# Five conv taps as four sums, some of them on GpSimd, with two heads in adjacent banks and an issue order written out

## The chip, the core and the metric

The kernel runs on one core of a Trainium2 chip. A core has TensorE (PE, with its weight loads shown apart as PEld), VectorE (DVE), ScalarE (ACT), GpSimd (POOL), and SyncE (SP), whose queue issues the DMAs. Each engine runs its own instructions in order; semaphores make one wait for another. The metric is device time in microseconds (us), the median of several runs. Next to it stands one profiled execution, from which all durations come.

## The reference

Batch 8, 8 heads, sequence 576, head width 64, all float32. Attention with a decay, then a gated linear unit whose gate is a causal convolution of five taps per channel:

```python
cum = np.cumsum(np.maximum(s, 0.0), axis=-1)
bias = -(cum[:, :, :, None] - cum[:, :, None, :])
scores = np.where(causal, -1000000000.0, scale * q @ k.T + np.minimum(bias, 0.0))
attn = softmax(scores)
x = (attn @ v)                       # heads side by side: (8, 576, 512)
for kk in range(5):
    gate_pre += conv_w[kk] * xp[:, kk:kk + S, :]      # xp: x with 4 zero rows in front
gate = 1.0 / (1.0 + np.exp(-gate_pre))
out = (gate * (x @ w_val)) @ w_out
```

## The kernel before

The work is cut into 32 steps n = 4b + p: batch b, and p, a pair of heads, which is also one chunk of 128 of the 512 channels. The decay factors into a weight on each row of v: `w = exp(cum - half)` multiplies v and a column of ones (`Vp`), so the scores need only exp and the causal mask, and the ones column gives the softmax denominator.

For one pair: `qk_T` transposes the bf16 q and k on TensorE and `qk_evac` (L516) copies them to `QKT`. `scores` (L521) computes the lower triangle in three steps of 512 columns (`STEPS`), each head in a bank of its own. In step 0, the diagonal blocks, four more matmuls with `sel` and `futA`/`futB` add -30000 above the diagonal (L563). `exps` (L566) runs one exp per head and step, from PSUM to `P` in bf16. `av` (L576) multiplies by `Vp`; `norm` takes two reciprocals (L583) and two products (L585), one of each per head. `x_T` transposes the result to channels by tokens in a PSUM bank, `x_evac` (L598) copies it to `xT` (four zero columns in front).

Then the convolution, `tap` (L600 to L612): tap 0 writes `gp = x * cwT[4]` over 576 columns, on DVE (L609) or, for odd n, on ACT (L607); taps 1 to 4 add `x` shifted by 1 to 4 columns times the other weights, all on DVE (L611), reading x from its PSUM bank. `tanh` (L616) gives the gate, `val` (L636) multiplies `xT` by `w_val`, `glu` (L642) forms `(tanh + 1) * val`, `outp` (L648) multiplies by half of `w_out`, `out_evac` (L653) copies to SBUF on ACT, and `store` writes out.

POOL builds constants at the start; later it casts q and k of batches 1 to 7 (L473) and their last 64 rows (L688), and multiplies Vp of these batches (L483). For batch 0 DVE and ACT do these steps. `w_val` and `w_out` are cast on DVE (L438).

The order comes from a planner, `Plan.run`: every task is added with an engine, an estimated duration, a due time (`DUE`), what it depends on and which buffers it takes (8 PSUM banks, 3 `P`, 2 `gp`, 6 `th`, 3 `ot`, 3 `qkf`). The planner simulates the five engines, picks for each the ready task that is due first, and the instructions are issued in the order that it finds. All DMAs go through SP's queue. At the end a small check counts rows whose softmax denominators are in range; unless all 128 are good, a second, general path runs as well.

Of the kernel before, what the change touches and what calls it, by code (L numbers as in the profile page):

```python
# [17 lines left out]
DM = 512  # L18
# [185 lines left out]
def pcol(kb, qb):  # L204
    if kb == qb:
        return kb * 128
    if qb == 4:
# [13 lines left out]

DUE = dict(av=1.08, norm=-15.2, xt=1.96, xe=-1.95, tap=2.26, dtap=0.21, tanh=3.88, cpe=-1.58, val=4.62,
           dval=0.97, out=12.49, dout=0.2, oute=12.42, qt=-3.05, qe=4.97, tt=-2, te=-24.47, s4=0.17,
           vp=-16.42, cast=4.1, lqk=-10.33, lv=-7.3)

STAY = (0.28, 13.36)

ON_PE = ()  # L230
PE_CHUNK = 2

ON_ACT = tuple(range(1, 32, 2))


class Plan:

    LAG = 0.2  # L240
    SWITCH = 0.18

    def __init__(self, bufs):
        self.bufs = bufs
        self.tasks = []
        self.slot = {}

    def add(self, eng, us, key, emit, deps=(), take=(), give=(), mode="N"):
        t = dict(eng=eng, us=us, key=key, emit=emit, deps=[d for d in deps if d is not None], take=take,
                 give=give, mode=mode, n=len(self.tasks), done=None)  # L250
        self.tasks.append(t)
        return t

    def run(self):
        engs = ["SP", "POOL", "PE", "ACT", "DVE"]
        free = {k: [(0.0, i) for i in range(n)] for k, n in self.bufs.items()}
        idle_at = dict.fromkeys(engs, 0.0)
        ready = {e: [] for e in engs}
        after = [[] for _ in self.tasks]
        for t in self.tasks:  # L260
            t["at"] = 0.0
            names = {d["n"] for d in t["deps"]}
            t["left"] = len(names)
            for i in names:
                after[i].append(t)
            if not names:
                ready[t["eng"]].append(t)
        mode, dma_free, now = "N", 0.0, 0.0
        self.order = []

        def can(t):

            at = t["at"]
            for kind in {kind for kind, _ in t["take"]}:
                c = sum(other == kind for other, _ in t["take"])
                if len(free[kind]) < c:
                    return None
                at = max(at, sorted(free[kind])[c - 1][0])
            return at

        while len(self.order) < len(self.tasks):
            started, later = False, []
            for e in engs:
                if idle_at[e] > now + 1e-9:
                    later.append(idle_at[e])
                    continue
                pick = None
                for t in ready[e]:
                    at = can(t)
                    if at is None:  # L290
                        continue
                    if at > now + 1e-9:
                        later.append(at)
                        continue
                    key = t["key"] + (STAY[t["mode"] == "N"] if e == "PE" and t["mode"] != mode else 0)
                    if pick is None or (key, t["n"]) < pick[:2]:
                        pick = (key, t["n"], t)
                if pick is None:
                    continue
                t = pick[2]  # L300
                us = t["us"]
                if e == "PE" and t["mode"] != mode:
                    us += self.SWITCH
                    mode = t["mode"]
                for kind, tok in t["take"]:
                    got = min(free[kind])
                    free[kind].remove(got)
                    self.slot[kind, tok] = got[1]
                t["start"] = now
                if e == "SP":  # L310
                    idle_at[e] = now + 0.06
                    dma_free = max(dma_free, now + 1.2) + us
                    t["done"] = dma_free + 0.8
                else:
                    idle_at[e] = t["done"] = now + us
                for kind, tok in t["give"]:
                    free[kind].append((t["done"] + self.LAG, self.slot[kind, tok]))
                ready[e].remove(t)
                self.order.append(t)
                later.append(idle_at[e])  # L320
                started = True
                for o in after[t["n"]]:
                    o["at"] = max(o["at"], t["done"] + (self.LAG if o["eng"] != e else 0.0))
                    o["left"] -= 1
                    if o["left"] == 0:
                        ready[o["eng"]].append(o)
            if not started:
                assert later
                now = min(later)
        return max(t["done"] for t in self.order)  # L330


def main_path(ctx, tc, q, k, v, s, moe_w_val, moe_conv_w, moe_w_out, out, okcnt):

# [5 lines left out]
    plan = Plan(dict(m=8, P=3, gp=2, th=6, ot=3, qkf=3))  # L343
    add, slot = plan.add, plan.slot

    def work(kind, tok, shape, dt):
        return one.tile(shape, dt, name=f"{kind}{slot[kind, tok]}")

    def bank(tok, shape, dt=FP32):
        return psum.tile(shape, dt, name=f"m{slot['m', tok]}")  # L350

    PE_CONV = lambda b, c: b in ON_PE and c == PE_CHUNK
    NS = B * 4

# [5 lines left out]
    vst = one.tile([128, NKB, 8, 65], FP32, name="vst")  # L360
    nc.gpsimd.memset(vst[:, :, :, 64:65], 1.0)
    nc.gpsimd.memset(vst[0:64, 4, :, :], 0.0)


    sel = one.tile([128, 2, 128], BF16, name="sel")
    nc.gpsimd.memset(sel, 0.0)
    futA = one.tile([128, 4, 64], BF16, name="futA")
    futB = one.tile([128, 4, 128], BF16, name="futB")
    nc.gpsimd.memset(futA, 0.0)
    nc.gpsimd.memset(futB, 0.0)  # L370
    for r0 in (0, 64):
        r = slice(r0, r0 + 64)
        for j in range(2):
            nc.gpsimd.tensor_copy(sel[r, j, 64 * j:64 * j + 64], ident[r, r])
        nc.gpsimd.affine_select(out=futA[r], in_=futA[r], pattern=[[0, 4], [1, 64]], compare_op=ALU.is_ge,
                                fill=NEG, base=0, channel_multiplier=-1)
        nc.gpsimd.affine_select(out=futB[r], in_=futB[r], pattern=[[0, 4], [1, 128]], compare_op=ALU.is_ge,
                                fill=NEG, base=-64, channel_multiplier=-1)
    P4s = [one.tile([128, 2, 4, 128], BF16, name=f"P4{j}") for j in range(2)]
    for P4 in P4s:  # L380
        nc.gpsimd.memset(P4[:, :, :, 0:64], 0.0)


    two = lambda name, shape, dt: [one.tile(shape, dt, name=f"{name}{j}") for j in range(2)]
    qkbs = [two("qb", [128, 4, 512], BF16), two("kb", [128, 4, 512], BF16)]
    tails, tailbs = two("tail", [128, 512], FP32), two("tailb", [128, 512], BF16)
    QKTs = two("QKT", [128, 2, 4, S], BF16)
    Vps = two("Vp", [128, NKB, 8, 65], BF16)
    xns = two("xn", [128, NKB, 512], BF16)
    xTs = two("xT", [128, 4, 4 + S], BF16)  # L390
    glus = two("glu", [128, 4, S], BF16)
# [9 lines left out]
    dg = one.tile([128, 15, 128], BF16, name="dg") if ON_PE else None  # L401
    for xT in xTs:
        nc.vector.memset(xT[:, :, 0:4], 0.0)


    t_s = add("SP", 0.8, -9, lambda: nc.sync.dma_start(out=sp, in_=s.rearrange("b h s -> (b h) s")))

    def relu():
        nc.vector.tensor_scalar(sp, sp, 0.0, None, ALU.max)

    def total():
        nc.vector.tensor_tensor_scan(cum, sp, sp, 0.0, ALU.add, ALU.max)

    def centre():
        nc.vector.tensor_scalar(chalf, cum[:, S - 1:S], 0.5, None, ALU.mult)  # L415
        nc.vector.tensor_scalar(cum, cum, chalf, None, ALU.subtract)

    def decay_T():
        pt = bank("w", [128, NKB, 64])
        slot["w"] = pt  # L420
        for i in range(NKB):
            nc.tensor.transpose(pt[:, i, :], cum[:, WIN[i]:WIN[i] + 128], identf)

    t = add("DVE", 0.65, -8, relu, [t_s])
    t = add("DVE", 1.3, -8, total, [t])
    t = add("DVE", 0.75, -8, centre, [t])
    t = add("PE", 1.2, -8, decay_T, [t], take=[("m", "w")])
    t_w = add("ACT", 0.5, -8, lambda: nc.scalar.activation(out=w, in_=slot["w"], func=AF.Exp), [t],
              give=[("m", "w")])


    t_wvo = []
    for nm, src, dst, sc, key in (("wv", moe_w_val, wv, 1.0, -5), ("wo", moe_w_out, wo, 0.5, -2.4)):
        def load(nm=nm, src=src):
            wt = slot[nm] = work("qkf", nm, [128, 4, DM], FP32)
            nc.sync.dma_start(out=wt, in_=src.rearrange("(c p) d -> p c d", c=4))
# [5 lines left out]
    def conv_T():  # L442
        pt = slot["cw"] = bank("cw", [128, 4, 5])
        for c in range(4):
            nc.tensor.transpose(pt[:, c, :], cw[:, c * 128:(c + 1) * 128], identf[0:5, 0:5])
# [416 lines left out]
```

## Time and profile before

| what | us |
|---|---|
| median of 3 runs (lowest to highest) | 227.53 (227.32 to 229.33) |
| span of the profiled execution | 228.0 |
| TensorE's mean granted clock there | 0.927 of full speed |

The profiled execution lies half a microsecond above the median. A profile page gives, for each engine, its busy time and share of the span, and the span in 40 slices, a digit being the busy tenths of a slice. Groups of instructions are given by line, engine and operation, with output and inputs by the program's names, shapes, count, busy time, the mean length of one, and the idle time of the engine just before them with what ended it. The chain of waits starts at the last instruction and goes back, at each step, to whatever released it. Instructions of an engine overlap at their ends, so a group's busy time is less than count times mean.

### The profile page before, as it was taken

The numbers are of one execution on the slowest core, as the hardware profiler recorded it, in microseconds if no ns is written. First come the engines' busy times: TensorE is split into PE (matmuls) and PEld (weight loads), VectorE is DVE, ScalarE is ACT, GpSimd is POOL, SyncE is SP. The second block draws the span as 40 slices with busy tenths as digits, with TensorE's granted clock in tenths as the row PEclk, the third lists the DMA queues.
The fourth block names the chain that finished last, engine by engine and source line by source line (L and its number), as shares of the span: only waits on it lengthen the run. The fifth ranks groups of instructions, "written<-read, shape, count | busy, mean of one in ns | idle before, by whom it ended". The sixth has DMA issues, their size and how long they took to land.

```text
span 228.0 us, 6320 instructions
## 1 busy us (share of the span) xinstructions
PE 194.5 (85%) x2561; PEld 129.0 (57%) x2561; DVE 190.3 (83%) x390; ACT 189.0 (83%) x348; POOL 73.4 (32%) x73
## 2 busy tenths in 40 slices
PE   0859876986999999998999699999999999899580
PEld 0547563573846756575657356765666566656220
DVE  3444459999899999999989979899899999999800
ACT  3698899925899999989999889899999989965340
POOL 8500622553873004959121770005305200000000
PEclk9965997697699999999999889999999999999887
DMA  5999999999994999599459121194291041044242
GB/s 152 240 274 329 270 170 299 298 176 195 358 249 141 207 325 297 155 253 377 175 131 267 45 69 49 35 203 135 115 230 29 3 184 26 3 159 162 96 149 74
DMA packets 69231, 40.50 MB, mean 178 GB/s; under 512 B 47109, under 2 KB 63493, under 8 KB 69194
## 3 DMA queue, kind: packets, MB, share of 16 engines
q1 hardware_dynamic: 69194, 40.01, 66.2%
q8 instruction: 22, 0.36, 0.6%
q14 instruction: 15, 0.12, 0.2%
HBM read 30.57 MB, written 9.44 MB: 175 GB/s over the span
## 4 chain that ended last, share of the span: by engine, by line
DVE 69%; PE 12%; SPq 8%; DMA 6%; issue 2%; ACT 1%; ACTq 0%
DVE gp L611 38%; DVE xn L585 10%; DVE glu L642 8%; DVE gp L609 5%; DMA qkf<-in_moe_w_val_dram 4%; DVE xT L598 4%; PE m L636 3%; PE m L648 3%; SPq L470 3%; SPq L478 2%; DVE recs L583 2%; SPq L489 2%; PE m L512 2%; PE m L576 1%; DMA out_dram<-ot 1%
## 5 line engine op out<-in xcount | busy, mean ns | idle before, releaser
L566 ACT ACTIVATE P<-m 128x512 bf16<-128x512 f32 x192 | 104.4, 672 | 11.0 <-PE m L563 9.1
L611 DVE SCALAR_TENSOR_TENSOR gp<-m,cwT,gp 128x572 f32<-128x572 bf16 (+3 forms) x128 | 102.9, 810 | 2.0
L521 PE MATMUL m<-QKT 64*128 64x128 bf16 (+4 forms) x576 | 45.8, 253 | 9.5 <-DVE xn L585 2.9
L483 POOL TENSOR_TENSOR Vp<-vst,w 128x650 bf16<-128x650 f32 x28 | 35.0, 1281 | 45.9 <-DMA vst<-in_v_dram 40.6
L636 PE MATMUL m<-xT,wv 128*128 128x288 bf16 x256 | 41.3, 293 | 2.8 <-DVE xn L585 0.8
L648 PE MATMUL m<-wo,glu 128*128 128x512 bf16 x160 | 41.9, 397 | 1.0 <-DVE gp L611 0.3
L521 PEld LDWEIGHTS <-QKT 64*128 64x128 bf16 x576 | 21.7, 98 | 31.4 <-issue 18.8
L576 PE MATMUL m<-Vp,P 128*128 128x65 bf16 x960 | 37.6, 197 | 1.8 <-ACT P L566 1.4
L576 PEld LDWEIGHTS <-P 128*128 128x128 bf16 x960 | 35.1, 100 | 5.6 <-ACT P L566 1.6
L516 ACT COPY QKT<-m 128x1024 bf16<-128x1024 bf16 x32 | 33.4, 1069 | 5.6 <-PE m L512 5.4
L653 ACT COPY ot<-m 128x512 f32<-128x512 f32 (+1 forms) x40 | 25.1, 651 | 9.4 <-PE m L648 6.7
L636 PEld LDWEIGHTS <-wv 128*128 128x128 bf16 x256 | 23.7, 99 | 13.8 <-issue 6.1
L642 DVE SCALAR_TENSOR_TENSOR glu<-th,m 128x288 bf16<-128x288 f32 x64 | 27.6, 445 | 1.4 <-PE m L636 1.4
L585 DVE TENSOR_TENSOR xn<-m,recs 128x320 bf16<-128x320 f32 x64 | 28.2, 482 | 0.0
L616 ACT ACTIVATE th<-gp 128x576 f32<-128x576 f32 x32 | 24.5, 767 | 1.6 <-DVE gp L611 1.6
L648 PEld LDWEIGHTS <-glu 128*128 128x128 bf16 x160 | 15.1, 101 | 18.1 <-issue 6.3
L473 POOL CAST qb<-qkf 128x2048 bf16<-128x2048 f32 x7 | 13.2, 1893 | 24.4 <-DMA qkf<-in_q_dram 16.2
L512 PE MATMUL m<-ident,qb 128*128 128x128 bf16 x128 | 13.9, 238 | 8.2 <-DVE chalf L415 6.1
L598 DVE COPY xT<-m 128x576 bf16<-128x576 bf16 x32 | 14.3, 449 | 5.1 <-PE m L594 5.1
L512 PEld LDWEIGHTS <-qb 128*128 128x128 bf16 x128 | 9.7, 107 | 11.7 <-DVE chalf L415 6.1
L594 PE MATMUL m<-ident,xn 128*128 128x128 bf16 x160 | 15.2, 230 | 1.1 <-ACT P L566 0.7
L473 POOL CAST kb<-qkf 128x2048 bf16<-128x2048 f32 x7 | 13.3, 1894 | 4.4 <-DMA qkf<-in_k_dram 4.4
(58 smaller groups left out, 154.1 us busy)
## 6 DMA issues: line engine op xcount, KB each, us to landing
out_dram<-ot SPq DMA_DIRECT2D x32, 256.0 KB, 2.2
qkf<-in_q_dram SPq DMA_DIRECT2D x7, 1024.0 KB, 9.8
qkf<-in_k_dram SPq DMA_DIRECT2D x7, 1024.0 KB, 9.0
vst<-in_v_dram SPq DMA_DIRECT2D x28, 256.0 KB, 5.0
vst<-in_v_dram SPq DMA_DIRECT2D x15, 128.0 KB, 4.6
first<-in_q_dram SPq DMA_DIRECT2D x4, 256.0 KB, 3.9
first<-in_k_dram SPq DMA_DIRECT2D x4, 256.0 KB, 4.0
tail<-in_q_dram SPq DMA_DIRECT2D x8, 128.0 KB, 9.3
```

The lines of the kernel that those rows point to most:

```text
L473: eng(qkbs[which][b % 2].rearrange("p j (h d) -> p h j d", h=8)[:, hs], f.rearrange("p h (j d) -> p h j d", j=4))
L483: eng.tensor_tensor(Vps[b % 2][:, :, h], vst[:, :, h], w[:, :, b * 8 + 2 * p:b * 8 + 2 * p + 2].unsqueeze(3).to_broadcast([128, NKB, 2, 65 ...
L512: nc.tensor.transpose(pt[:, which, j * 128:(j + 1) * 128], qkbs[which][b % 2][:, j, p * 128:(p + 1) * 128], ident)
L516: nc.scalar.copy(QKTs[b % 2][:, :, p, 0:512].rearrange("d w (x j) -> d w x j", j=4), slot["qt", b, p].rearrange("d w (j x) -> d w x j", j=4))
L521: nc.tensor.matmul(ps[hh][:, c0:c0 + nq], QKTs[b % 2][r, 1, p, k0:k0 + 128], QKTs[b % 2][r, 0, p, q0:q0 + nq], **kw)
L566: nc.scalar.activation(out=slot["Pt", n][:, hh, step * 512:(step + 1) * 512], in_=slot["s", n, step][hh], func=AF.Exp, scale=0.125)
L576: nc.tensor.matmul(ps[:, qb * 65:qb * 65 + 65], lhsT, Vps[b % 2][:, kb, 2 * p + hh, :], start=(kb == 0), stop=(kb == qb))
L585: nc.vector.tensor_tensor(xns[b % 2][:, :, p * 128 + hh * 64:p * 128 + hh * 64 + 64], pvs[hh][:, :, 0:64], recs[:, n, hh].unsqueeze(2).to_ ...
L611: nc.vector.scalar_tensor_tensor(gp[:, sh:S], x[:, 0:S - sh], cwT[:, c, 4 - sh:5 - sh], gp[:, sh:S], ALU.mult, ALU.add)
L636: nc.tensor.matmul(ps, wv[:, dc, c * 128:(c + 1) * 128], xTs[b % 2][:, dc, 4 + o:4 + o + 288], start=(dc == 0), stop=(dc == 3))
L642: nc.vector.scalar_tensor_tensor(glus[b % 2][:, c, o], slot["t", n][:, o], 1.0, slot["v", n, hf], ALU.add, ALU.mult)
L648: nc.tensor.matmul(ps, glus[b % 2][:, c, WIN[i]:WIN[i] + 128], wo[:, c, :], start=(c == 0), stop=(c == 3))
```

## The change

The planner, its due times and its buffers by name go. An `ORDER` text of tokens `step.indices:engine:slots` takes their place: the engine is S, G (GpSimd), T (TensorE), A or V, and the slots name PSUM banks and buffers. A loop issues the steps in this order. Loads, casts and evictions may name any engine.

```diff
-DUE = dict(av=1.08, norm=-15.2, xt=1.96, xe=-1.95, tap=2.26, dtap=0.21, tanh=3.88, cpe=-1.58, val=4.62,
...
-ON_ACT = tuple(range(1, 32, 2))
-class Plan:
...
+BUFS = {'vst': 1, 'P': 3, 'gp': 4, 'th': 5, 'ot': 4, 'qkf': 3, 'qkw': 2048}
+ORDER = """
...
+t3.7:G ld_v.3.3:S s1.10:T:6 rec.8:V nm.8:V val.6.1:T:1 e1.10:A ld_v.3.2:S s2.10:T:2 oe.0.2:V:0 xt.8:T:4 e2.10:A
+mk.10:G glu.6.1:V s0.11:T:6:2 ld_v.3.0:S val.7.0:T:5 xe.8:V e0.11:A t1.8:V:0 s1.11:T:0 st.0.2:S s2.11:T:2 ld_q.4:S:0
...
+t1.30:V:2 st.6.0:S t2.30:V out.6.3:T:2 oe.6.1:A:3 st.6.1:S xe.31:V out.6.4:T:1 th.29:A:0 t3.30:G t1.31:V:0
+oe.6.3:A:0 out.6.2:T:0 t2.31:V oe.6.4:A:1 st.6.3:S val.30.0:T:2 st.6.4:S t4.30:G oe.6.2:A:2 t3.31:V val.30.1:T:1
...
+"""
+    with tc.manual_schedule():
+        for name, e, *slots in steps:
+            f, *ix = name.split(".")
...
+            does[f](engines[e], *ix)
```

The weights of the convolution become ratios to the last one, whose half becomes the scale of tanh. A sum on GpSimd is two instructions, since GpSimd reads `xT` from SBUF and has a product and an addition apart:

```diff
+    def conv_ratio(e):
+        vec.tensor_copy(cwT, bank[:, at["cwT"][0], 0:20].rearrange("p (c k) -> p c k", c=4))
+        vec.reciprocal(cwi, cwT[:, :, 4:5])
+        vec.tensor_tensor(cwr[:, :, 0:4], cwT[:, :, 0:4], cwi.to_broadcast([128, 4, 4]), ALU.mult)
+        vec.tensor_scalar(cwr[:, :, 4:5], cwT[:, :, 4:5], 0.5, None, ALU.mult)
...
-        if m == 0:
-            if n in ON_ACT:
-                nc.scalar.activation(out=gp, in_=x, func=AF.Copy, scale=cwT[:, c, 4:5])
-            else:
-                nc.vector.tensor_scalar(gp, x, cwT[:, c, 4:5], None, ALU.mult)
-        else:
-            nc.vector.scalar_tensor_tensor(gp[:, sh:S], x[:, 0:S - sh], cwT[:, c, 4 - sh:5 - sh], gp[:, sh:S],
-                                           ALU.mult, ALU.add)
+            if m == 1:
+                vec.scalar_tensor_tensor(gp, xT[:, 3:3 + S], r, xps(n), ALU.mult, ALU.add)
+            elif e is vec:
+                vec.scalar_tensor_tensor(gp[:, m:S], xps(n)[:, 0:S - m], r, gp[:, m:S], ALU.mult, ALU.add)
+            else:
+                pool.tensor_scalar(prod[:, m:S], xT[:, 4:4 + S - m], r, None, ALU.mult)
+                pool.tensor_tensor(gp[:, m:S], gp[:, m:S], prod[:, m:S], ALU.add)
...
+        act.activation(out=ths[at["th", n][0]], in_=gps[at["t1", n][0]], func=AF.Tanh, scale=cwr[:, n % 4, 4:5])
```

PSUM becomes one tile of eight banks, in which the scores of both heads, and both attention outputs, lie in two adjacent banks. One exp, one reciprocal and one product then cover both heads. Where the order has a step `mk` for a pair, the four mask matmuls of its step 0 are left out, and GpSimd sets the upper triangles of `P` to zero after the exp:

```diff
+    def pair(tok):
+        j = at[tok][0]
+        return bank[:, j:j + 2, :]
...
+            masked = step == 0 and mk[n] == 0
...
-            nc.vector.reciprocal(recs[:, n, hh], pvs[hh][:, :, 64])
+        vec.reciprocal(recs[:, n], pair(("av", n))[:, :, 0:325].rearrange("t w (g d) -> t w g d", d=65)[:, :, :, 64])
...
-        nc.scalar.activation(out=slot["Pt", n][:, hh, step * 512:(step + 1) * 512], in_=slot["s", n, step][hh],
-                             func=AF.Exp, scale=0.125)
+            act.activation(out=Pt(n)[:, :, step * 512:(step + 1) * 512], in_=pair((f"s{step}", n)), func=AF.Exp,
+                           scale=0.125)
+    def mask(e, n):
+        d = Pt(n)[:, :, 0:512].rearrange("k w (g q) -> k w g q", g=4)
+        pool.affine_select(out=d, in_=d, pattern=[[0, 2], [0, 4], [1, 128]], compare_op=ALU.is_ge, fill=0.0, base=0,
+                           channel_multiplier=-1)
```

The steps whose engine the order chooses, counted from before and from the `ORDER` text:

| step | before | after |
|---|---|---|
| scaling tap | 16 DVE, 16 ACT | none |
| sums t1 to t4 (32 each) | 128 DVE | 82 DVE (32, 32, 14, 4), 46 GpSimd (t3 18, t4 28) |
| pairs masked | 32 PE | 17 PE, 15 GpSimd |
| QKT evictions | 32 ACT | 20 ACT, 12 DVE |
| tail evictions | 8 ACT | 3 ACT, 5 DVE |
| tail casts | 1 DVE, 7 GpSimd | 5 DVE, 3 GpSimd |
| Vp products | 4 DVE, 28 GpSimd | 17 DVE, 15 GpSimd |
| casts of batch 0's q and k, by pair | 4 DVE, 4 ACT | 1 DVE, 4 ACT, 3 GpSimd |
| casts of w_val, w_out | 2 DVE | 1 GpSimd, 1 DVE |
| output copies | 40 ACT | 34 ACT, 6 DVE |

The check at the end is split: one part covers the first 28 pairs and the squares of the ratios (at most 1e12), the other the last four pairs.

## The prediction, on record before the changed kernel ran

> **What bounds the kernel now.** I read the page's busy line and slices first, to see which engine is full, then the busy times of three stretches (start, middle, end), then the chain of waits, then the groups and the timeline for prices.
>
> ```profile
> PE 194.5 (85%) x2561; PEld 129.0 (57%) x2561; DVE 190.3 (83%) x390; ACT 189.0 (83%) x348; POOL 73.4 (32%) x73
> DVE  3444459999899999999989979899899999999800
> POOL 8500622553873004959121770005305200000000
> ```
>
> Three engines look alike at 83 to 85%, but DVE's slices are at eight or nine from the seventh on but for two, and POOL is mostly idle. The stretches (time, then each engine's busy time) show why:
>
> ```profile
> 0.00:31.30 31.30, 20.58 (x286) 16.02 (x287) 12.57 (x30) 22.53 (x45) 12.40 (x27) 0.84 0.97 244
> 31.30:213.80 182.50, 167.73 (x2257) 110.59 (x2254) 175.74 (x356) 163.57 (x299) 60.95 (x46) 0.95 0.65 173
> 213.80:228.00 14.20, 6.16 (x22) 2.35 (x22) 1.97 (x6) 2.92 (x5) 0.00 (x0) 0.78 0.28 95
> ```
>
> In the middle DVE (third pair) works 175.74 of 182.50 us, 96%. Its idle time is 31.30-12.57 = 18.7 us at the start, 6.8 in the middle and 12.2 at the end: 37.7, and 190.3+37.7 = 228.0, the span. I forecast in this form. The chain agrees (shares of the span), and its pieces give a tap's price:
>
> ```profile
> DVE 69%; PE 12%; SPq 8%; DMA 6%; issue 2%; ACT 1%; ACTq 0%
> ```
> ```profile
> 207.00 0.73 DVE gp L611
> 207.75 0.82 DVE gp L611
> ```
>
> A tap holds DVE 0.73 us before an independent instruction and 0.82 before one that needs its result (about 0.84 with the gap).
>
> **Prices.** Groups: busy, mean ns of one | idle before.
>
> ```profile
> L566 ACT ACTIVATE P<-m 128x512 bf16<-128x512 f32 x192 | 104.4, 672 | 11.0 <-PE m L563 9.1
> L611 DVE SCALAR_TENSOR_TENSOR gp<-m,cwT,gp 128x572 f32<-128x572 bf16 (+3 forms) x128 | 102.9, 810 | 2.0
> L483 POOL TENSOR_TENSOR Vp<-vst,w 128x650 bf16<-128x650 f32 x28 | 35.0, 1281 | 45.9 <-DMA vst<-in_v_dram 40.6
> L585 DVE TENSOR_TENSOR xn<-m,recs 128x320 bf16<-128x320 f32 x64 | 28.2, 482 | 0.0
> L473 POOL CAST kb<-qkf 128x2048 bf16<-128x2048 f32 x7 | 13.3, 1894 | 4.4 <-DMA qkf<-in_k_dram 4.4
> L609 DVE TENSOR_SCALAR gp<-m,cwT 128x576 f32<-128x576 bf16 x16 | 12.9, 808 | 0.0
> L563 PE MATMUL m<-futB,sel 64*128 64x512 bf16 x64 | 13.9, 411 | 0.0
> L563 PE MATMUL m<-futA,sel 64*128 64x256 bf16 x64 | 9.9, 288 | 0.0
> ```
>
> **Four sums for five taps.** The last weight moves into the tanh scale, so the tap that only multiplied goes: 16 on DVE (12.9 us) and 16 on ACT (13.2 us busy). Of the 128 sums the written order leaves 82 on DVE (32 t1, 32 t2, 14 t3, 4 t4) and gives 46 to GpSimd. DVE's taps were 102.9+12.9 = 115.8 us; the 82 left mostly stand right behind what they need, so 82 x 0.84 = 68.9: 46.9 saved (45 to 50, at 0.73 and 0.81 for each of the 62 gone). t1 now reads xT just written, so x_evac's tail shows: 32 x 0.1 = 3 us back.
>
> A sum on GpSimd is a product (one input) and an addition (two). The addition by the Vp row, 1281/650 = 1.97 ns per element, is 1.13 us. The product has no row: from below the cast (1894/2048 = 0.92 ns, 0.53 us), from above the addition's 1.13. It has one input and one output like the cast, so I take 0.65: 1.78 us for both (1.66 to 2.26), 46 of them 82 us.
>
> **Heads in adjacent banks.** 64 reciprocals become 32: 8.9/2 = 4.4 us of DVE. 64 norms become 32 of 640 elements: glu's 288 take 445 ns and the norm's 320 take 482, so 1.16 ns per element; 0.85 us each, 0.80 behind overlap, 25.6 for 28.2: 2.6 saved. Two exps of 512 become one of 1024. Timeline rows of six exps and of three 1024-wide copies:
>
> ```profile
> 23.97 3.04 ACT L566 ACTIVATE P<-m 128x512 bf16<-128x512 f32 x6 [0.48 <-PE m L521]
> ```
> ```profile
> 102.19 2.84 ACT L516 COPY QKT<-m 128x1024 bf16<-128x1024 bf16 x3 [0.95 <-PE m L512]
> ```
>
> One exp more costs (3.04-0.59)/5 = 0.49, one wide copy more (2.84-1.05)/2 = 0.89: at best 0.09 per pair, 8.6 us of ACT; I take 6. It is hidden: ACT is not the bound. What it costs is that the exp waits for both heads' scores.
>
> **Mask.** 15 of 32 pairs drop four mask matmuls: (13.9+9.9)/32 = 0.74 us each, 11 us of PE. GpSimd pays one select over 1024 elements; this trace's select of 512 took 0.84-0.85 us, so 1.7 each, 25 us, with the attention products of that pair queued behind it. Three P buffers and other pairs' matmuls cover it; uncovered, it is 15 x 1.7 = 25 us, held in the high end.
>
> **Moves.** To DVE: 13 Vp (0.77 us each, 10.0), 12 QKT evictions (strided; 0.8 us by xT's 449 ns for 576, 1.4 by the taps' rate; 1.0 taken, 12.0), 6 output copies (0.7, 4.2), 5 tail evictions and 4 tail casts (0.5 and 0.42, 4.2), checks 1.5. Off DVE: the wv cast and three first casts, 2.5. SP issues the same loads in another order, up to a batch ahead; it is no bound (DMA share 0.65 in the middle).
>
> **Sums.** DVE: 190.3-46.9+3-4.4-2.6+10.0+12.0+4.2+4.2+1.5-2.5 = 168.8 (163 to 176). ACT: 189.0-13.2-6, less 12 evictions (12), 5 tails (3), 6 outputs (4) and the halved last-block exps (1): 150. PE: 183. GpSimd: set-up 7.3, 15 Vp 19.2, 15 big casts 28.4, six small casts 4, masks 25, sums 82: 166 (160 to 188).
>
> One resource has no clean row. Two copies on POOL took 0.40 us alone and 1.58 while DVE's scan (two SBUF inputs, 4.10 to 5.76) ran:
>
> ```profile
> 2.99 0.40 POOL L374 COPY sel<-ident 64x64 bf16<-64x64 bf16 x2
> ...
> 4.60 1.58 POOL L374 COPY sel<-ident 64x64 bf16<-64x64 bf16 x2
> ```
>
> So an encounter costs up to the DVE instruction's length. New on DVE with SBUF sources alone are the 13 Vp and 4 tail casts, 12 us of encounters at most, none at best; I take half, on GpSimd, off the bound. The taps, norms and gates read PSUM beside one SBUF tensor, and POOL's Vp beside such taps were all 1.28 us. By the Trainium skill, "SBUF — State Buffer", section "Who interferes with whom", a VectorE instruction with two SBUF inputs and a reading GpSimd instruction exclude each other, whoever starts second waiting; the rows agree.
>
> **The span.** DVE's start idle 18.7 held 3.57 us waiting for the wv load:
>
> ```profile
> 31.26 1.23 DVE L438 TENSOR_SCALAR wv<-qkf 128x2048 bf16<-128x2048 f32 x1 [3.57 <-DMA qkf<-in_moe_w_val_dram]
> ```
>
> That cast goes to GpSimd, and the written order starts taps while the first batch is still arriving: 15. Middle: 6.8 grows, since four engines are now between 73 and 90%: 8. End 12 as before (the last output group, copies and stores stay). 168.8+15+8+12 = 203.8, and the median stands 0.5 under the profiled span: 203.3 us. Bounds: 163+13+6+11 = 193 below.
>
> **Rivals.**
> *GpSimd sets the pace.* For it: 32% becomes some 80%, in order, with casts that wait for loads ahead of sums. Span = set-up 8.7 + wait for the first big load 8 + 77 other work + 46c + 15 behind the last tap = 108.7+46c. At c = 1.78 it is 191, under my forecast; at 2.26 it is 213, with 10 us of encounters and waits 222. By the Trainium skill, "GPSIMD Engine Reference", section "Engine selection", two-input elementwise work belongs on VectorE, GpSimd being about twice as slow; it speaks against the move, and the rows (1.97 against 810/572 = 1.4 ns) agree in direction.
> *Slower than before.* The same queue, if each sum costs over (230-108.7)/46 = 2.64 us: t4 gates tanh, the gate product and the output, so DVE and PE starve; at 2.8 us 237. Against it: 2.64 is 0.38 above my upper price.
> *Better packing.* If the early taps fill the start (idle 10) and DVE's evictions run at 0.8: 166+10+6+11 = 193, less 0.5.
> *Nothing gained.* The fixed order loses in waits what the work gains (24 us): about 227. DVE at 96% under the old order shows that order can be good; nothing shows it must be. Also, if a ratio were too large the second, general path would run, far slower; the largest drawn is 306, the limit 1e6.
>
> **Chances.** Forecast (196 to 209) 0.57; GpSimd's pace (209 to 222) 0.18; better packing (188 to 196) 0.14; nothing gained 0.04; slower 0.07, the general path among it. A change of 1%, 2.3 us, is what a measurement can tell. Faster 0.89, same 0.04, slower 0.07. The range 192 to 217 takes the forecast, most of GpSimd's case and some of the better one.
>
> **What would show it.** DVE near 169 us and its middle at 90% or more; one exp near 0.9 us; product and addition near 0.65 and 1.13; POOL near 166. Wrong if DVE idles on POOL in the middle, if POOL's casts wait on loads with taps behind them, or if PE waits on masks.

## The result, and the profile after

| what | us |
|---|---|
| before, median of the runs beside it | 228.43 |
| after, median of 4 runs (lowest to highest) | 262.85 (262.42 to 264.94) |
| ratio after to before, 95% interval | 1.155 (1.147 to 1.164) |
| predicted, and its range | 203.3 (192 to 217) |
| span of the profiled execution after | 260.9 (TensorE's mean granted clock 0.937) |

Some executions come out over 1.5% above the fastest of the same kernel; the ratios leave these out, the medians do not. The change made the kernel 15.5% slower. The forecast was a gain of 11%, so its sign was wrong. The busy line and the slices of the changed kernel:

```profile
PE 188.0 (72%) x2482; PEld 127.2 (49%) x2501; DVE 183.3 (70%) x308; ACT 161.6 (62%) x202; POOL 225.0 (86%) x167
...
DVE  1536899997999999747536863699737789569130
...
POOL 8655999996999999999999999849999999999900
```

The two rows have changed places. POOL, mostly idle before, stands at nine in nearly every slice from the fifth to the thirty-eighth. DVE, full before, now falls to three and five in the middle. The middle stretch, from 31.3 us to the end of the last sum on POOL (time, length, then the busy time of PE, PEld, DVE, ACT and POOL):

```profile
31.30:248.00 216.70, 164.27 (x2204) 111.33 (x2221) 165.26 (x273) 138.92 (x173) 203.33 (x132) 0.93 0.53 145
```

POOL works 203.33 of 216.70 us, 94%; DVE 165.26, 76%, where it had 96% before. The chain of waits says the same, DVE's share having gone from 69% to 9%:

```profile
POOL 49%; PE 11%; SPq 10%; issue 9%; DVE 9%; DMA 8%; ACT 1%; POOLq 0%; ACTq 0%; DVEq 0%
```

The groups that matter (count | busy, mean ns of one | idle time before them and what ended it):

```profile
L620 POOL TENSOR_SCALAR prod<-xT,cwr 128x572 f32<-128x572 bf16 (+1 forms) x46 | 83.1, 1807 | 2.6
L621 POOL TENSOR_TENSOR gp<-gp,prod 128x572 f32<-128x572 f32 (+1 forms) x46 | 65.3, 1421 | 6.5 <-DVE gp L618 2.3
L575 POOL TENSOR_SCALAR_AFFINE_SELECT P<-P 128x1024 bf16<-128x1024 bf16 x15 | 17.6, 1170 | 5.4 <-ACT P L569 5.4
L625 ACT ACTIVATE th<-gp,cwr 128x576 f32<-128x576 f32 x32 | 24.8, 778 | 54.9 <-POOL gp L621 54.8
L569 ACT ACTIVATE P<-bank 128x1024 bf16<-128x1024 f32 x96 | 94.1, 1028 | 14.9 <-PE bank L518 10.1
L493 DVE TENSOR_TENSOR Vp<-vst,w 128x650 bf16<-128x650 f32 x17 | 18.4, 1098 | 3.1 <-DMA vst<-in_v_dram 3.1
```

The product takes 1.81 us, the addition 1.42. Tanh (fourth row) has been held up for 54.9 us, all but 0.1 of it by POOL's additions: the last sum stands ahead of the gate. POOL's own rows of the timeline (start, length) show the pace of its queue:

```profile
106.61 1.73 POOL L620 TENSOR_SCALAR prod<-xT,cwr 128x573 f32<-128x573 bf16 x1
108.43 1.40 POOL L621 TENSOR_TENSOR gp<-gp,prod 128x573 f32<-128x573 f32 x1
109.92 1.72 POOL L620 TENSOR_SCALAR prod<-xT,cwr 128x572 f32<-128x572 bf16 x1
...
113.21 1.72 POOL L620 TENSOR_SCALAR prod<-xT,cwr 128x573 f32<-128x573 bf16 x1
```

Three products start 3.30 us apart, with no wait listed between: one undisturbed sum takes 3.30 us of the queue. Put into the formula of the two rivals on GpSimd's queue, 108.7 + 46 x 3.30 = 260.5 us. The span is 260.9; how much of this agreement is luck is worked out further down.

### The profile page after: what moved, and what is told of

Same layout as the page of the kernel before. It is cut to its first block, busy times and chain, and to the rows that moved or that the text cites. A ratio compares the mean times of both kernels' runs of the same rounds, so it can differ in the third digit from the quotient of the medians.

```text
span 260.9 us, 6228 instructions
## 1 busy us (share of the span) xinstructions
PE 188.0 (72%) x2482; PEld 127.2 (49%) x2501; DVE 183.3 (70%) x308; ACT 161.6 (62%) x202; POOL 225.0 (86%) x167
## 4 chain that ended last, share of the span: by engine, by line
POOL 49%; PE 11%; SPq 10%; issue 9%; DVE 9%; DMA 8%; ACT 1%; POOLq 0%; ACTq 0%; DVEq 0%
POOL prod L620 21%; POOL gp L621 16%; PE bank L632 5%; SPq L490 4%; DMA tail<-in_k_dram 3%; POOL P L575 3%; POOL Vp L493 3%; DMA qkf<-in_k_dram 3%; POOL qb L396 3%; POOL kb L396 3%; SPq L458 2%; SPq L475 2%; DVE xn L595 2%; DMA out_dram<-ot 1%; PE bank L509 1%
## 5 line engine op out<-in xcount | busy, mean ns | idle before, releaser
L569 ACT ACTIVATE P<-bank 128x1024 bf16<-128x1024 f32 x96 | 94.1, 1028 | 14.9 <-PE bank L518 10.1
L620 POOL TENSOR_SCALAR prod<-xT,cwr 128x572 f32<-128x572 bf16 (+1 forms) x46 | 83.1, 1807 | 2.6
L621 POOL TENSOR_TENSOR gp<-gp,prod 128x572 f32<-128x572 f32 (+1 forms) x46 | 65.3, 1421 | 6.5 <-DVE gp L618 2.3
L625 ACT ACTIVATE th<-gp,cwr 128x576 f32<-128x576 f32 x32 | 24.8, 778 | 54.9 <-POOL gp L621 54.8
L518 PE MATMUL bank<-QKT 64*128 64x128 bf16 (+4 forms) x576 | 40.2, 251 | 23.9 <-ACT P L569 13.6
L632 PE MATMUL bank<-xT,wv 128*128 128x288 bf16 x256 | 44.6, 318 | 11.0 <-ACT ot L396 7.1
L643 PE MATMUL bank<-wo,glu 128*128 128x512 bf16 x141 | 40.1, 401 | 7.8 <-DVE glu L638 3.5
L638 DVE SCALAR_TENSOR_TENSOR glu<-th,bank 128x288 bf16<-128x288 f32 x64 | 27.2, 446 | 23.9 <-PE bank L632 14.5
L586 PE MATMUL bank<-Vp,P 128*128 128x65 bf16 x960 | 38.4, 199 | 6.2 <-POOL P L575 2.5
L618 DVE SCALAR_TENSOR_TENSOR gp<-bank,cwr,gp 128x574 f32<-128x574 bf16 (+2 forms) x50 | 40.5, 812 | 1.2
L595 DVE TENSOR_TENSOR xn<-bank,recs 128x640 bf16<-128x640 f32 x32 | 26.3, 823 | 0.9
L608 DVE COPY xT<-bank 128x576 bf16<-128x576 bf16 x32 | 14.4, 451 | 12.9 <-PE bank L604 12.9
L575 POOL TENSOR_SCALAR_AFFINE_SELECT P<-P 128x1024 bf16<-128x1024 bf16 x15 | 17.6, 1170 | 5.4 <-ACT P L569 5.4
L493 DVE TENSOR_TENSOR Vp<-vst,w 128x650 bf16<-128x650 f32 x17 | 18.4, 1098 | 3.1 <-DMA vst<-in_v_dram 3.1
```

The source lines that it names most:

```text
L493: e.tensor_tensor(Vps[b % 2][:, :, HP[p]], vslot(b)[:, :, HP[p]], w[:, :, b * 8 + 2 * p:b * 8 + 2 * p + 2].unsqueeze(3).to_broadcast([128, ...
L518: pe.matmul(ps[:, hh, c0:c0 + nq], QKTs[b % 2][r, 1, p, k0:k0 + 128], QKTs[b % 2][r, 0, p, q0:q0 + nq], **kw)
L569: act.activation(out=Pt(n)[:, :, step * 512:(step + 1) * 512], in_=pair((f"s{step}", n)), func=AF.Exp, scale=0.125)
L586: pe.matmul(ps[:, qb * 65:qb * 65 + 65], lhsT, Vps[b % 2][:, kb, 2 * p + hh, :], start=(kb == 0), stop=(kb == qb))
L595: vec.tensor_tensor(xns[b % 2][:, :, p * 128:(p + 1) * 128].rearrange("t g (w d) -> t w g d", w=2), pair(("av", n))[:, :, 0:325].rearrange ...
L618: vec.scalar_tensor_tensor(gp[:, m:S], xps(n)[:, 0:S - m], r, gp[:, m:S], ALU.mult, ALU.add)
```

## The experiments

**The theory and its rivals.** The theory after the result: GpSimd's queue sets the time because a sum costs 3.30 us there, and the product is what was mis-sized. Rivals: the 15 masks on GpSimd; the written order and the paired banks, which would be slow whatever GpSimd does; the steps that were moved to VectorE. The first experiment asks why the product is dear.

**Four forms of the product.** In the changed kernel the four chunks of channels were given four forms:

```diff
-                pool.tensor_scalar(prod[:, m:S], xT[:, 4:4 + S - m], r, None, ALU.mult)
+                if c == 0:
+                    pool.tensor_scalar(prod[:, m:S], xT[:, 4:4 + S - m], r, None, ALU.mult)
+                elif c == 1:
+                    pool.tensor_scalar(prod[:, m:S], xT[:, 4:4 + S - m], 0.25, None, ALU.mult)
+                elif c == 2:
+                    pool.tensor_tensor(prod[:, m:S], xT[:, 4:4 + S - m], r.to_broadcast([128, S - m]), ALU.mult)
+                else:
+                    pool.tensor_scalar(prod[:, m:S], gp[:, m:S], r, None, ALU.mult)
```

> GpSimd's product is made in four forms by channel chunk: as it is (a scale per partition, bf16 in), with a constant scale, as a product of two tensors with the scale broadcast, and with a scale per partition but float32 in. The gate is wrong in two of the chunks. If the scale per partition is what makes the product cost 1.72 us instead of the 0.65 that I took, the constant form takes 0.5 to 0.7, the broadcast form 1.1 to 1.4, the float32 form stays at 1.7. If it is the bf16 input or the float32 output, the constant form stays near 1.7 too, and a float32 input alone may change it. If encounters with DVE lengthen it, all forms spread alike.

Groups of that kernel, shapes kept apart (L621 is the form of the change, L623 the constant, L627 the float32 input, L625 the product of two tensors):

```profile
L623 POOL TENSOR_SCALAR prod<-xT 128x572 f32<-128x572 bf16 x7 | 12.5, 1784 | 0.4
L621 POOL TENSOR_SCALAR prod<-xT,cwr 128x572 f32<-128x572 bf16 x7 | 12.5, 1781 | 0.5
L627 POOL TENSOR_SCALAR prod<-gp,cwr 128x572 f32<-128x572 f32 x6 | 10.4, 1741 | 3.8 <-DVE gp L618 3.5
L625 POOL TENSOR_TENSOR prod<-xT,cwr 128x572 f32<-128x572 bf16 x8 | 9.2, 1151 | 0.4
```

The time was that of after, 263.0 us in one run. The means of the rows hold a few products that a Vp product on VectorE lengthened (2.10 us at 100.98, beside one from 99.68 to 101.58); the median is 1.72 us for the form of the change and for the float32 input, 1.65 for the constant and 1.14 for the product of two tensors with the scale broadcast. So neither the scale held per partition nor the bf16 input makes the one-input multiplication dear: it takes 1.65 to 1.72 us in all three forms, about 3 ns per element. The float32 output alone does not either, since the broadcast form has it too. Why the form with a scalar is dear stays open; none with a bf16 output was timed. By the Trainium skill, "GPSIMD Engine Reference", section "Engine selection", it is the two-input operation that is slow on GpSimd, and a one-input operation runs at roughly line rate. These rows say the reverse for this operation, and the rows decide.

**All products in that form.**

```diff
-                pool.tensor_scalar(prod[:, m:S], xT[:, 4:4 + S - m], r, None, ALU.mult)
+                pool.tensor_tensor(prod[:, m:S], xT[:, 4:4 + S - m], r.to_broadcast([128, S - m]), ALU.mult)
```

> The changed kernel with its 46 products made as products of two tensors, the scale broadcast, which the look at the four forms showed at 1.15 us where the change takes 1.7 to 1.8. Nothing else moves. If GpSimd's queue sets the pace, its work falls by 46 x 0.6 = 27 us to some 198 and the time by 20 to 27 us, to 236 to 243. If the order's own waits set it, under 10 us are gained.

Measured: 243.0 us, ratio 1.070 (1.061 to 1.080). The group of products:

```profile
L620 POOL TENSOR_TENSOR prod<-xT,cwr 128x572 f32<-128x572 bf16 (+1 forms) x46 | 55.6, 1208 | 3.2 <-DVE xT L608 1.2
```

The products' busy time fell from 83.1 to 55.6 us, 27.5, and the time by 19.9. Putting one operation another way, on the same engine and with the same result, wins back over half of the 34.4 us that after loses to before. POOL is still 83% busy. The formula is less good here: sums start 2.70 us apart where nothing disturbs them, 108.7 + 46 x 2.70 = 233, and the span is 240.5.

**The products on ScalarE.** Three product buffers in turn, and an activation in place of the product:

```diff
-                pool.tensor_scalar(prod[:, m:S], xT[:, 4:4 + S - m], r, None, ALU.mult)
+                act.activation(out=prod[:, m:S], in_=xT[:, 4:4 + S - m], func=AF.Copy, scale=r)
```

> The 46 products go from GpSimd to ACT (a copy with a scale), each addition stays on GpSimd; three prod buffers for one. If GpSimd's queue sets the pace: its work falls by 46 x 1.8 = 83 us to 142, ACT's rises by 46 x 0.65 = 30 to 191, DVE stays at 183, and the time falls to 215 to 230. If the written order's waits set the pace whatever GpSimd does, the time stays above 245.

Measured: 233.65 us, ratio 1.027 (1.018 to 1.036), above the 215 to 230 expected. The busy line:

```profile
PE 180.2 (78%) x2501; PEld 122.2 (53%) x2501; DVE 183.8 (80%) x308; ACT 189.9 (82%) x248; POOL 142.0 (62%) x121
```

POOL lost 83.0 us of work and the time 29.2. Here GpSimd is no longer the bound (the formula would give 108.7 + 46 x 1.4 = 173), and yet the kernel is slower than before. So GpSimd's full queue explains the way from 262.9 to about 234, not the way from there to the forecast.

**The masks back on TensorE.** The 15 `mk` steps are taken out of the order, so the mask matmuls of these pairs are issued again:

```diff
-s2.0:T:2 c_q.0.1:A mk.0:G ld_q.0.3:S
+s2.0:T:2 c_q.0.1:A ld_q.0.3:S
```

> All 32 pairs are masked on PE, none on GpSimd. If GpSimd's queue sets the pace: 17.6 us of selects and some 5 us of idle time ahead of them leave it, PE gains 15 x 0.74 = 11 us and has room; the time falls by 15 to 23 us, to 240 to 248. If PE or the order sets the pace, it stays within 5 us of 262 or rises.

Measured: 255.95 us, ratio 1.123 (1.115 to 1.131): 6.9 us faster than after, where 15 to 23 were expected, although POOL's work fell from 225.0 to 205.5. The rest went into waits in POOL's queue: ahead of the products it waits 11.2 us, 8.3 of them for VectorE's copy `xT`, where after had 2.6. The queue is the bound only as long as it always has something ready.

**All sums on VectorE, every move undone (batch 0's casts and Vp apart).** The sequence of the steps, the banks and the masks stay as in the change; only engines differ. The 46 sums read `xT` in SBUF, since their PSUM bank is given away earlier:

```diff
-t4.0:G
+t4.0:V:9
-qe.0.2:V
+qe.0.2:A
-vp.1.2:V
+vp.1.2:G
...
+            elif (f"t{m}", n) in at:
+                vec.scalar_tensor_tensor(gp[:, m:S], xT[:, 4:4 + S - m], r, gp[:, m:S], ALU.mult, ALU.add)
             elif e is vec:
```

> All 128 sums on DVE, and the evictions, casts and Vp products that went to DVE back on ACT and GpSimd (batch 0 apart); the four sums, the adjacent banks, the 15 masks on GpSimd and the places in the written order stay. If GpSimd's queue was the whole loss: GpSimd falls to some 95 us, DVE is at 183 + 46 x 0.84 - 15 (Vp) - 14 (QKT) - 9 (the rest) = 184, and the time is 215 to 225, under the 228 of before. If the written order loses by its own waits, DVE has more than 15 us of idle time in the middle and the time is above 235.

Measured: 238.19 us, ratio 1.036 (1.025 to 1.047). The same with all masks on TensorE as well:

> All sums on DVE, every move undone, and all masks on PE; four sums, adjacent banks and the written order stay. In the run with the masks on GpSimd, GpSimd stood 50.8 us ahead of masks, waiting for the exp, with casts and Vp products queued behind. If that queue is what cost the 10 us over the kernel before, the time falls to 222 to 230. If the written order costs by itself, it stays within 4 us of 238, and DVE still idles 50 us.

Measured: 234.16 us, ratio 1.029 (1.022 to 1.037). So of the 15.5% by which the changed kernel is slower than before, giving sums to GpSimd and what was moved for it is worth 12 points, some 27 us (ratio 1.155 to 1.036). The masks are worth under one point (1.036 to 1.029), and those two intervals overlap, so a price of theirs is not shown. What is left is 3 points, 7 us, and whatever gain four sums should have brought. In the last of these kernels, by the stretches, the middle reads:

```profile
31.30:220.00 188.70, 160.99 (x2263) 108.20 (x2279) 165.32 (x275) 153.44 (x192) 66.94 (x47) 0.97 0.62 167
```

VectorE idles 188.70 - 165.32 = 23.4 us of the middle with GpSimd far from full. Before it was 6.8. VectorE's work holds a cost of its own here, too:

```profile
L615 DVE SCALAR_TENSOR_TENSOR gp<-xT,cwr,gp 128x572 f32<-128x572 bf16 (+1 forms) x46 | 45.7, 995 | 0.1
L617 DVE SCALAR_TENSOR_TENSOR gp<-bank,cwr,gp 128x574 f32<-128x574 bf16 (+2 forms) x50 | 40.4, 811 | 1.1
```

The first row is the 46 sums that now read `xT` and `gp` in SBUF, the second those that read x in PSUM. Their medians are alike, 0.81 and 0.82 us. But none of the second row takes over 0.82, and ten of the first take 1.08 us and more, 2.54 at most; one of 1.72 started at 120.87, in a stretch in which GpSimd made four Vp products (118.84 to 124.97). These are encounters as in the prediction, on VectorE's side: 46 x (0.995 - 0.811) = 8.5 us.

**Was it the merged instructions?** From that kernel, first the exps were split again into one per head, then reciprocals and products of the attention outputs too; the banks stay in pairs:

```diff
-            act.activation(out=Pt(n)[:, :, step * 512:(step + 1) * 512], in_=pair((f"s{step}", n)), func=AF.Exp,
-                           scale=0.125)
+            for hh in range(2):
+                act.activation(out=Pt(n)[:, hh, step * 512:(step + 1) * 512], in_=pair((f"s{step}", n))[:, hh, :],
+                               func=AF.Exp, scale=0.125)
```

> The run with every sum on DVE, the moves undone and the masks on PE (234.2 us), with each exp of both heads split into one per head again; banks, order and all else stay. If the hand-over of both banks at once is what adjacent banks cost, the time falls by 4 to 8 us, although ACT gains up to 9 us of work. If merging only saved ACT work, the time stays or rises by up to 5 us.

> As the run with the exps split, and the reciprocals and norms split per head too; what is left of adjacent banks is where they lie. If the hand-over per pair is the cost, this falls further, to within 4 us of the kernel before with four sums (224.4). If the cost is in the written order or in pairs of banks as a unit of allocation, it stays above 230; DVE has 32 more reciprocals and norms, 7 us, to carry.

Measured: 235.80 (ratio 1.038, 1.030 to 1.045) and 236.24 us (1.039, 1.029 to 1.049). It is not the merging, since splitting gains nothing over 1.029.

**Four sums alone.** The planner's kernel of before, with its banks and buffers, and only the ratios and the four sums, all on VectorE. The planner works out a new order for it, since tasks are gone and a sum is estimated at 0.78 us instead of 0.73:

```diff
-        if m == 0:
...
+        if m == 1:
+            nc.vector.scalar_tensor_tensor(gp, xTs[b % 2][:, c, 3:3 + S], r, x, ALU.mult, ALU.add)
...
-                for m in range(5):
+                for m in range(1, 5):
```

> The kernel before, planner and all, with only the four sums by ratios (all on DVE; no scaling tap on DVE or ACT). DVE's work falls by 12.9 us less up to 3 for the sum that waits on xT, to 177 to 181, ACT's by 13.2 to 176. As DVE was the bound: 216 to 222 us. If the sum that waits on xT costs more than thought, or PE at 194 takes over, the time is 223 to 228.

Measured: 224.43 us over 10 runs, ratio 0.989 (0.985 to 0.994): 2.7 us faster than the before beside it. Busy line and chain:

```profile
PE 185.5 (83%) x2544; PEld 125.2 (56%) x2561; DVE 180.6 (81%) x377; ACT 181.4 (81%) x332; POOL 73.9 (33%) x73
...
DVE 35%; PE 24%; ACT 20%; SPq 8%; DMA 6%; issue 3%; ACTq 0%; DVEq 0%
```

DVE's work fell by 9.7 us and the span of the profiled execution by 5.3. In the chain DVE's 69% became 35%, with PE and ACT at 24 and 20, so the chain now passes through three engines by turns. That would explain why only a part of the 9.7 us came back: the bound was only a few us ahead of the next two. The new order is a rival that this run does not part from it; the runs below show how much an order can be worth.

**Paired banks in the planner's order.** Three kernels start from the one just shown. First all scores and attention outputs in pairs (two pairs of banks and four single ones, the instructions merged):

```diff
-    plan = Plan(dict(m=8, P=3, gp=2, th=6, ot=3, qkf=3))
+    plan = Plan(dict(m=4, mp=2, P=3, gp=2, th=6, ot=3, qkf=3))
```

> The kernel before with the planner, the four sums, and the heads in adjacent banks (two pairs of banks for scores and attention outputs, four single banks), all masks on PE, nothing on other engines than before: the same work as the run with the moves undone and the masks on PE, in an order that the planner finds. If the written order is what loses, it is near or under 220 us, DVE idling some 40 us. If adjacent banks cost (an exp waits for both heads, two pairs of banks in turn), it is above the run of the kernel before with four sums alone by more than 4 us.

Measured: 235.89 us, ratio 1.036 (1.027 to 1.045). That is close to the written order's 234.2: with paired banks and all sums on VectorE in both, the written order does not show worse than this order of the planner's. Then each half of it alone, the attention outputs in one pair (`m=6, mp=1`), or the scores in two pairs (`m=4, mp=2`):

> The planner's kernel with four sums, and only the two attention outputs of a pair of heads in adjacent banks (one pair of banks and six single ones), with one reciprocal and one product for both; scores and exps stay one head to a bank. VectorE's work falls by 4 to 6 us. If pairs as such cost the 11 us of the run with all of them paired, it is at 230 or above; if the paired scores cost them, at 220 to 225.

> The other half: only the scores of a pair of heads in adjacent banks (two pairs and four single banks), with one exp for both; the attention outputs stay one head to a bank. ScalarE's work falls by 4 to 8 us. If paired scores cost the 11 us, it is at 232 to 238; if the cost comes from the attention outputs and the scores having to share the two pairs, at 222 to 228.

Measured: 260.26 (ratio 1.143, 1.136 to 1.149) and 247.53 us (1.090, 1.085 to 1.095). Either half alone is worse than both together, which neither expectation foresaw. So the loss can't be put down to one of the two uses. What the three have in common is that eight banks are divided into kinds that can't stand in for one another, and that the planner works out another order from it; these runs don't part the two. With one pair for all attention outputs, VectorE's reciprocal waited 35.4 us for TensorE's attention products, the longest time 10.4. (The written order names banks one by one and isn't divided so; whether any of its 10 us over 224.4 comes from the pairs isn't shown.)

**Sums on GpSimd that is not full.** Still from the kernel with four sums alone, the last sum of 16 pairs, and of 8, went to GpSimd as a broadcast product and an addition, with four `gp` and five `th`:

```diff
+            if m == 4 and ON_POOL(n):
+                nc.gpsimd.tensor_tensor(prod[:, m:S], xTs[b % 2][:, c, 4:4 + S - m], r.to_broadcast([128, S - m]),
+                                        ALU.mult)
+                nc.gpsimd.tensor_tensor(gp[:, m:S], gp[:, m:S], prod[:, m:S], ALU.add)
+                return
```

> The kernel before with the planner and four sums, and the last sum of the 16 odd pairs on GpSimd as a broadcast product and an addition (1.15 + 1.40 us), with four gp buffers for two and five th for six. GpSimd rises from 74 to 115 us, DVE falls from 181 to 168. If GpSimd is harmless while far from full: 214 to 221 us. If any GpSimd step on the way to the gate costs (casts and Vp ahead of it in its queue), 224 or more.

> The same with 8 pairs instead of 16. If GpSimd is harmless while far from full: halfway, 218 to 223 us. If its steps cost, it lies nearer 224 than the run with 16.

Measured: 235.45 (ratio 1.031, 1.022 to 1.041) and 231.80 us (1.023, 1.017 to 1.030). This looked like a price of late sums on GpSimd even where it is half idle. That reading fell with the next three kernels: the buffers changed alone, and the sums moved with the buffers as they were (two and six).

> The planner's kernel with four sums, all on VectorE, and only its buffers changed: four gp and five th in place of two and six, as in the runs with 16 or 8 last sums on GpSimd (235.5 and 231.8). If the GpSimd sums cost there what they cost over 224.4, this run stays at 223 to 226; if it was the planner's order with other buffers, it comes out at 230 or more.

> The planner's kernel with four sums and the last sum of the 16 odd pairs on GpSimd (broadcast product and addition), now with the buffers as they were: two gp, six th. If the 11 us that this step cost came from the buffers, it is at 222 to 228 beside 224.4 with all sums on VectorE; if two gp buffers hold up the next pair while GpSimd adds, or GpSimd's place on the way to the gate costs, at 232 or more.

> The same with 8 pairs (every fourth), two gp and six th. Between 220 and 226 if a few sums fit into GpSimd's free time and VectorE's 6 us less count; 228 or more if one late sum on GpSimd holds up the gate whatever the buffers.

| kernel | sums on GpSimd | gp, th | us | ratio to before (95%) |
|---|---|---|---|---|
| four sums alone | 0 | 2, 6 | 224.43 | 0.989 (0.985 to 0.994) |
| buffers alone | 0 | 4, 5 | 235.04 | 1.035 (1.031 to 1.040) |
| 16 sums | 16 | 4, 5 | 235.45 | 1.031 (1.022 to 1.041) |
| 8 sums | 8 | 4, 5 | 231.80 | 1.023 (1.017 to 1.030) |
| 16 sums | 16 | 2, 6 | 224.02 | 0.981 (0.974 to 0.989) |
| 8 sums | 8 | 2, 6 | 240.53 | 1.056 (1.050 to 1.063) |

The buffers alone cost 10.6 us, and with equal buffers 16 sums on GpSimd cost nothing (ratios 1.031 against 1.035, 0.981 against 0.989). With 8 it is 3 us faster with one set of buffers and 16 slower with the other. The planner works out a new order at every such edit. Each number of sums on GpSimd stands twice in the table, with the same instructions, other buffers and another order; the two differ by 9 to 11 us, and not always the same way. So a single planner run can't price a part of this change to better than that. This holds for the three kernels with paired banks as well, and for the 2.7 us of four sums alone. The busy line of the 16 sums with the old buffers:

```profile
PE 186.0 (84%) x2561; PEld 126.9 (57%) x2561; DVE 170.9 (77%) x361; ACT 181.1 (82%) x332; POOL 114.1 (51%) x105
```

It is, with the four sums alone, one of the two kernels that beat both before and after; their intervals overlap. VectorE has 9.7 us less to do than in the four sums alone and the time is the same: in these two orders VectorE's work alone does not set it.

## Why the prediction was wrong

**The step that failed** is the price of a sum on GpSimd: "I take 0.65: 1.78 us for both (1.66 to 2.26)". The product measured 1.81 us on average (1.72 undisturbed, which here is the median of the group), the addition 1.42 (1.40), and an undisturbed sum took 3.30 of the queue. The product was taken near the cast because it has one input and one output like it, with the addition as its upper end. Both rows were of other operations, and neither was a bound: undisturbed, the product takes 1721/572 = 3.0 ns per element and the addition 1397/572 = 2.4, against 0.92 of the cast and 1.97 of the Vp product. The error is 46 x (3.30 - 1.78) = 70 us of GpSimd's queue: some 49 from the product, 12 from the addition, 8 from the gaps between instructions, which the sum had at nothing. At 1.78 the formula left that queue 191 us, 12 below the forecast; the 70 us used those 12 up and set the time from there. The Vp row, a product of two tensors, does give the price of the broadcast form: 1140/572 = 2.0 ns. What had no row was the form with a scalar that the change used.

**The rival that came true** is "Slower than before", with the place (t4 gates tanh) confirmed. It had a chance of 0.07 because 2.64 lay 0.38 above "my upper price". That upper price was the weak link: it was the slowest row at hand, not a limit of the operation that had no row. The deciding point of 2.64 us was itself too high: with the broadcast product an undisturbed sum takes 2.70, for which the formula gives 233, and that kernel measured 243.0, 7% slower than before.

That the formula gives 260.5 for a span of 260.9 is partly luck. GpSimd's set-up ended at 7.5 us (8.7 taken), its other work came to 218.3 - 148.4 = 69.9 (77), and 12.9 us stood behind the last sum (15): 10.4 us less than the formula has. The sums and all idle time between took 148.4 + 22.2 = 170.6 us, where the formula has 151.8 + 8 = 159.8: 10.8 more. Of the other work a mask took 1.17 rather than 1.7 us (17.6 for 25), while Vp and the casts took a little more.

**VectorE's work** came out at 183.3 us rather than 168.8, outside the range of 163 to 176. Rows that account for most: Vp 17 x 1.10 rather than 0.77 (18.4 us for 13), reciprocals 6.9 for 4.4, the moved evictions and tail casts 16.5 and 3.5 for 14.5 and 2.1, checks and ratios about 3 more. The taps were right or better (66.5 us for 68.9). Part of the rest is probably overlap: the groups of before add up to 207 us over 190.3 of busy time, those of after to 194 over 183.3, so taking instructions out can save less than their groups' busy time.

**The encounters** were about right. A Vp product on VectorE and a product on GpSimd, both on SBUF alone:

```profile
148.82 0.83 DVE L493 TENSOR_TENSOR Vp<-vst,w 128x650 bf16<-128x650 f32 x1
148.88 2.35 POOL L620 TENSOR_SCALAR prod<-xT,cwr 128x572 f32<-128x572 bf16 x1
```

The product grows from 1.72 by 0.63. Over the trace, (1.807 - 1.721) x 46 + (1.170 - 1.10) x 15 + (1.411 - 1.28) x 15 = 7 us on GpSimd, where 6 were taken; but they lay on the bound, not off it. Vp on VectorE, 0.83 alone, reached 2.03, 1.10 on average; the sum had not counted encounters on that side.

**The merged exps** gave more than the 6 us taken: 94.1 us of ScalarE for 104.4. It was hidden, as said. That TensorE would wait for masks came to 2.5 us.

**The span's form**, VectorE's work plus idle time much like before (35 us), does not hold in the kernels below: GpSimd is the bound in none of them, and idle time is 42 us and more in all but before. So cheap sums alone need not have brought the forecast about. VectorE's busy and idle time by kernel:

| kernel | busy | idle | span |
|---|---|---|---|
| before | 190.3 | 37.7 | 228.0 |
| four sums alone | 180.6 | 42.1 | 222.7 |
| 16 sums on GpSimd, planner | 170.9 | 51.3 | 222.2 |
| after, products on ScalarE | 183.8 | 47.1 | 230.9 |
| after, all back, masks on TensorE | 184.0 | 50.2 | 234.2 |

Of 19.4 us less work on VectorE (first and third row) the span gained 5.8. The sum took "Middle 8" on the ground that four engines would be between 73 and 90% busy; it is 23.4 in the last row. That ScalarE and TensorE stood at 83 and 85% beside VectorE's 83 was read off the page and came into the sum with 1.2 us only (8 for 6.8). The rival *Nothing gained*, at 227 with a chance of 0.04, is what remains of the change when GpSimd is relieved, and some 7 us worse.

**What stays open:** what makes up the 10 us between 224.4 (four sums alone) and 234.2 (all back, masks on TensorE). The pairs of banks, the written order and the 46 sums that read SBUF beside GpSimd (8.5 us of VectorE's time) are three candidates. A fourth is that 224.4 is a lucky order: the planner's kernel with the same instructions and other buffers is at 235.0. A written order with single banks wasn't tried, nor one in which the 46 sums read PSUM.

## What to carry to other kernels

When the only price for a moved operation comes from rows of other operations, the slowest of them is no upper bound: work out the price at which the move turns against you, and if that is near the rows, the chance of it is large. An engine at 32% is free for what it has been seen to do at a known price, and a step ahead of a gate turns its queue into everybody's. And where three engines stand within two per cent of one another, take work off one and do not count on all of it coming back (of 19.4 us, 5.8 here, in one order of the planner's). Before pricing a part by a run of its own, see how far two runs with the same work and another order lie apart: here it was 10 us.

## What the runs showed of the hardware that was not expected

- GpSimd's multiplication by a scalar takes 1.65 us (constant) to 1.72 us (scale per partition) for 572 elements when undisturbed, about 3 ns per element, with bf16 or float32 input; the product of two tensors with a broadcast scale takes 1.14 us, 2.0 ns.
- The float32 addition of two tensors takes 1.40 us there undisturbed, 2.4 ns per element, beside 1.97 of the Vp product.
- A select over 1024 bf16 elements on GpSimd takes 1.10 us undisturbed, where two of 512, on 64 partitions, took 1.7 in the trace of before.
- VectorE's sum takes the same 0.81 us with both inputs in SBUF as with one of them in PSUM, but only the former is lengthened while GpSimd works: ten of 46 took 1.08 to 2.54 us, none of 50 over 0.82 (the kernel with everything back and the masks on TensorE).
